# Weight pieces of an attention-and-experts kernel copied by VectorE or ScalarE as the list scheduler places them, with other weights for its due times

## The chip, the cores and the metric

The kernel runs on one core of one Trainium2 chip. The metric is the device time of one execution in microseconds (us), the median of several runs; lower is better. The engines are named as in the profile: PE is TensorE's matmul side and PEld its weight load, DVE is VectorE, ACT is ScalarE, POOL is GpSimd and SP is SyncE, which issues most DMAs here.

## The reference

Two parts follow one another. The first is an attention over channels, for 4 batches of 5056 tokens with 256 channels; the second is a mixture of 8 experts on its 20224 output rows, each row going to the expert with the highest gate logit.

```python
qn = q / (norm(q, axis=1) + 1e-6); kn = k / (norm(k, axis=1) + 1e-6)
s = kn.transpose(0, 2, 1) @ qn / tau            # 256 x 256 for each batch
a = softmax(s)
x = (v @ a).reshape(B * N, C)                   # 20224 x 256
logits = x @ w_gate; e = argmax(logits)         # 8 experts
out[row] = gate_w * (relu(x[row] @ w1[e]) @ w2[e])   # 256 -> 1024 -> 256
```

## The kernel before, in words

**The expert blocks.** Rows that the attention has produced are scattered by POOL to a DRAM array `xs` that has a region for each expert. Whenever a stage of the attention is complete (`ENDS`, L33: after some groups of 512 tokens, two in batch 0 and three in each later batch), a table (L509 on) is computed that says which expert and which 256 rows each of the next blocks takes. There are 72 blocks of 256 rows in 11 stages (`SURE` is 5, 12, 18, 26, 32, 38, 46, 52, 58, 66, 72 blocks, counted up) and 18 blocks of 128 rows for the rest. A block (L615 on) loads its rows transposed (`xT`, L609) and a small tile `mt` (L611) by SP, and multiplies in float16 parts: every number is a high and a low half, and three products stand for one.

**The pieces.** All weights lie in SBUF as float16 halves in `W`. Which expert a block needs is known on the chip alone, so its weights are copied from `W` at a register's address into a tile `wp` of 128 x 1024 (`piece`, L627): 8 pieces a block, 4 for the first matrix product (`first`, L631, PE L640 into PSUM tile `hp`) and 4 for the second (`second`, L655, PE L664 into `y`). The register is loaded once a block by `expert` (L621). There are 5 `wp` buffers (`WP`), so a piece can be made when PE has finished with the piece five back. In the kernel before, every piece is a VectorE copy (L629). ScalarE takes the ReLU of `hp` into the high half of `ht` (L648), VectorE makes the low half (L651), ScalarE scales `y` into `o` (L678) and POOL scatters `o` to the output (L682).

**The side work.** While the blocks of one stage run, the attention of the next groups goes on beside them: loads of q and k chunks, norms (`nraw`, ACT L1274, 20 loads of 512 KB for each of batches 1 to 3), halves of the chunks (`hl`, ACT L168 and DVE L175), score products (`sp`, PE L205 and L206), a softmax of small steps for each batch, and for each group of 512 tokens four products `px` (PE L1142), copies `xg` (ACT L1148), squares (ACT L1154), rows (ACT L364, DVE L368), the choice of the expert (DVE L388 to L398), counts (`r_ex`, DVE L411 and L412), ranks (`rtp`, PE L417 and L420) and four scatters (POOL L456).

**What sets the order.** All engines run in order, and the order is made ahead of time by a list scheduler (`task` L703, `lay` L717): every step is a task with an engine, a planned cost in us, the tasks it needs and a rank. `lay` repeatedly takes the task that could begin first by the planned times; among tasks that could begin at once, the one with the lower rank. A task is begun as soon as its engine is free and its inputs are there, so the rank only says who goes first; it holds nothing back. A piece is planned at 0.45 us of VectorE, `expert` at 0.4. PE's steps that read another engine's result are planned 0.4 us behind it, some 1.0 us (`LEAD`).

**The due times.** The ranks are due times. L973 to L1008 give every step of side work a weight (for a group of batch 1 to 3: 4 x 1.9 for its products and 0.5 for its rank), add these up, and spread them over the numbered blocks so that a stage's weights are done `EARLY` = 2 blocks before its rows are wanted (a hull of points of block number and summed weight). A step's due time (`due`, L1017) is read off that line; a block's steps have theirs from the block's number (`block_due`, L1020).

Of the kernel before, what the change touches and what calls it, by code (L numbers as in the profile page):

```python
# [18 lines left out]
ENG = mybir.EngineType  # L19

P = 128
B, N, C = 4, 5056, 256
NP = 5120
E, F = 8, 1024
# [5 lines left out]
T = 4  # L30
# [38 lines left out]
def attention_then_experts(ctx, tc, qk, qkc, vT, wts_in, kc, out):  # L69
# [89 lines left out]
    WP = 5  # L159
# [454 lines left out]
    def block(stage, tab, i, load):  # L614
        nt = P if stage == LAST else BLK  # L615
        nj = nt // P
        nf = 512 // nt
        wps, hps, hts, ys = {}, {}, {}, []
        b = {}

        def expert():  # L621
            b["e"] = nc.values_load(
                tab()[0][0:1, i : i + 1], engines=[ENG.DVE], min_val=0, max_val=E - 1,
                skip_runtime_bounds_check_because=WHY,
            )

        def piece(n):  # L627
            wps[n] = work.tile([P, 1024], F16, tag="wp", name="wp", bufs=WP)
            vec.tensor_copy(out=wps[n], in_=Wf[:, ds(b["e"] * 8192 + n * 1024, 1024)])  # L629

        def first(k):  # L631
            wp = wps.pop(k).rearrange("p (d s f) -> p d s f", d=2, s=2)
            xT = load()[0]
            for f in (2 * k, 2 * k + 1):
                if f % nf == 0:
                    hps[f // nf] = ps_h.tile([P, nf, nt], F32, tag="hp", name="hp")
                n = 0
                for dc in range(2):
                    for wh, xh in ((0, 0), (0, 1), (1, 0)):
                        pe.matmul(  # L640
                            hps[f // nf][:, f % nf, :], wp[:, dc, wh, (f % 2) * P : (f % 2 + 1) * P],
                            xT[:, 2 * xh + dc, :], start=(n == 0), stop=(n == 5),
                        )
                        n += 1

        def relu(h):
            hts[h] = work.tile([P, 2, nf, nt], F16, tag="ht", name="ht", bufs=4)
            act.activation(hts[h][:, 0], hps[h], AF.Relu)  # L648

        def rest(h):  # L650
            vec.scalar_tensor_tensor(  # L651
                out=hts[h][:, 1], in0=hps.pop(h), scalar=0.0, in1=hts[h][:, 0], op0=ALU.max, op1=ALU.subtract
            )

        def second(k):  # L655
            if k == 0:
                both = ps_y.tile([P, 2, C], F32, tag="y", name="y", bufs=2)
                ys.extend(both[:, j, :] for j in range(nj))
            wp = wps.pop(4 + k).rearrange("p (f s d) -> p f s d", f=2, s=2)
            for f in (2 * k, 2 * k + 1):  # L660
                for j in range(nj):
                    n = 0
                    for hh, wh in ((0, 0), (0, 1), (1, 0)):
                        pe.matmul(  # L664
                            ys[j], hts[f // nf][:, hh, f % nf, j * P : (j + 1) * P], wp[:, f % 2, wh, :],
                            start=(f == 0 and j == 0 and n == 0), stop=(f == 7 and j == nj - 1 and n == 2),
                        )
                        n += 1

        def factor():  # L670
            b["fac"] = tiny.tile([P, 2], F32, name="b_fac")[:, 0:nj]
            vec.tensor_scalar(
                out=b["fac"], in0=load()[1][:, :, 0], scalar1=fe[:, ds(b["e"], 1)], scalar2=None, op0=ALU.mult
            )

        def result(j):
            b["o", j] = work.tile([P, C], F32, tag="o", name="o", bufs=2)
            act.activation(b["o", j], ys[j], AF.Copy, scale=b["fac"][:, j : j + 1])  # L678

        def store(j):  # L680
            stored(
                pool.indirect_dma_start(  # L682
                    out=out[:, :],
                    out_offset=bass.IndirectOffsetOnAxis(ap=load()[1].bitcast(I32)[:, j, 1:2], axis=0),
                    in_=b.pop(("o", j)), in_offset=None, bounds_check=NT - 1, oob_is_err=False,
                )
            )

        return nj, nf, expert, piece, first, relu, rest, second, factor, result, store
# [8 lines left out]
                    tc.declare_no_dep(raw, group=f"bank{t2}{other.engine}", reason="another bank")  # L698
        tc.add_to_no_dep_group(f"bank{t}{raw.engine}", raw)

    tasks, rings = {}, {}

    def task(name, engine, cost, deps, emit, rank, after=0.0, wire=0.0, takes=(), uses=(), on=()):  # L703
        deps = list(deps)
# [12 lines left out]
    def lay():  # L717
        needs, users = {}, {}
        for name, (_, _, deps, *_) in tasks.items():
            flat = set()  # L720
            for d in deps:
                flat.update(d if isinstance(d, list) else [d])
            flat.discard(name)
            for d in flat:
                users.setdefault(d, []).append(name)
            needs[name] = flat
        missing = [d for d in users if d not in tasks]
        assert not missing, missing
        open_, ready, free, ends, begun = {n: len(d) for n, d in needs.items()}, {}, {}, {}, []
        wire = 0.0  # L730

        def made_ready(name):
            engine = tasks[name][0]
            at = 0.0
            for d in needs[name]:
                end, other, seen = ends[d]
                at = max(at, end if other is engine else seen + (LEAD.get(name[:2], LEAD.get(name[0], 0.4)) if engine is pe else 0.0))
            ready.setdefault(engine, {})[name] = at

        for name, n in open_.items():  # L740
            if n == 0:
                made_ready(name)
        while any(ready.values()):
            best = None
            for engine, some in ready.items():
                now = free.get(engine, 0.0)
                for name, at in some.items():
                    key = (max(at, now), tasks[name][4], len(begun))
                    if best is None or key < best[0]:
                        best = (key, name)  # L750
            (at, _, _), name = best
            engine, cost, deps, emit, rank, after, carried = tasks[name]
            del ready[engine][name]
            end = at + cost
            if engine is not None:
                free[engine] = end
            seen = end + (0.25 if engine is pe else 0.12) + after
            if carried:
                wire = max(wire, end + after) + carried
                seen = wire + 0.6  # L760
            ends[name] = (end, engine, seen)
            begun.append((at, len(begun), name))
            for u in users.get(name, ()):
                open_[u] -= 1
                if open_[u] == 0:
                    made_ready(u)
        assert len(begun) == len(tasks), [n for n in tasks if n not in ends][:20]
        for _, _, name in sorted(begun):
            tasks[name][3]()
        return begun, ends  # L770

    by_hand = tc.manual_schedule(engines={pe.engine, act.engine, vec.engine, sync.engine})
# [68 lines left out]
    def call(f, *args):  # L841
        return lambda: f(*args)
# [136 lines left out]
    for b in range(B):  # L979
        side = []  # L980
        if b == 1:
            side += [(("norm", b, n), 0.0, 0.6) for n in range(20)]
        if b > 1:
            side += [(("chunk", b, ch), 1.31, 1.2) for ch in range(NCH)]
        if b:
            side += [(("soft", b), 3.0, 7.0)]
        for g in range(AHEAD if b == 0 else 0, G):
            side += [(("x", b, g, t), 0.68 if b else 0.89, 1.9 if b else 1.2) for t in range(T)] + [(("rank", b, g), 0.3, 0.5)]
        for what, cost, weight in side:
            amount[what] = total  # L990
            total += weight
            done_by.append(total)
            spent.append(spent[-1] + cost)
            if what[0] == "rank" and what[1:] in ENDS[1:]:
                bounds.append(total)
# [356 lines left out]
    def block_tasks(n):  # L1352
# [15 lines left out]
        many = 8 // nf  # L1368
        for k in range(4):
            yield  # L1370
            task(("piece", n, k), vec, 0.45, [("expert", n)], call(piece, k), d(2 * k + 1) - 2, takes=[("wp", WP)])
            opens, closes = 2 * k % nf == 0, (2 * k + 1) % nf == nf - 1
            task(("first", n, k), pe, whole, [("piece", n, k), ("load", n), "handed"] + ([("first", n, k - 1)] if k else []),
                 call(first, k), d(2 * k + 1), takes=[("hp", 3)] if opens else [], uses=[("wp", 0)] + ([] if opens else [("hp", 0)]))
# [6 lines left out]
        task(("factor", n), vec, 0.14, [("load", n), ("expert", n), "factors"], factor, d(10), takes=[("b_fac", 2)], on=[mts])  # L1381
        for k in range(4):
            yield
            task(("piece", n, 4 + k), vec, 0.45, [("expert", n)], call(piece, 4 + k), d(8 + 2 * k) - 2, takes=[("wp", WP)])
            h = (2 * k + 1) // nf
            task(("second", n, k), pe, 1.32 if nj == 2 else 0.66, [("piece", n, 4 + k), ("rest", n, h)] + ([("second", n, k - 1)] if k else []),
                 call(second, k), d(8 + 2 * k), takes=[("y", 2)] if k == 0 else [], uses=[("wp", 0)])
            hts[h].append(("second", n, k))
# [80 lines left out]
```

## Time and profile before

| | us |
|---|---|
| median of 3 runs | 1175.9 (1173.66 to 1176.03) |
| the profiled execution, its own time | 1175.05 |
| its span, first to last instruction | 1173.3 |
| PE busy | 1136.9 (97%) |
| DVE busy | 903.8 (77%) |
| ACT busy | 673.2 (57%) |
| POOL busy | 358.8 (31%) |

The busy times are unions of what each engine executed; waiting, register loads and semaphores are not in them. A matmul's recorded end lies behind the moment at which the next one may start, so an idle gap of PE looks somewhat shorter in the profile than the time that was lost.

### The profile page before, as it was taken

The page shows a single profiled execution, that of the slowest core. Times are in us where ns is not written, and L with a number is a line of the kernel's source. Part 1 is how long each engine was busy: PE and PEld are TensorE (multiplying, and loading weights), DVE is VectorE, ACT ScalarE, POOL GpSimd, SP SyncE. Part 2 cuts the span into 40 slices and gives each one's busy share as a digit, 9 for nine tenths or more (in the row PEclk, how much of TensorE's full clock was granted, in tenths as well). Part 3 has the DMA queues.
Part 4 walks back from the last instruction along what each step waited for, and adds up shares of the span by engine and source line. Part 5 has one row for each costly group of instructions (what it writes and reads, how often), then busy time and mean ns, then how long its engine had stood idle before and what let it go on. Part 6 is the DMA issues. An engine that isn't in the chain of part 4 may idle for free.

```text
span 1173.3 us, 28744 instructions
## 1 busy us (share of the span) xinstructions
PE 1136.9 (97%) x10325; PEld 992.6 (85%) x10325; DVE 903.8 (77%) x2624; ACT 673.2 (57%) x1475; POOL 358.8 (31%) x335
## 2 busy tenths in 40 slices
PE   9989999989999999999999999999999999999998
PEld 8878778878888777988878877888888888889997
DVE  5797676877778887787768797778788677767886
ACT  5575476577876555477776655466565443332332
POOL 0044432234343411143344321133343323322222
PEclk9999899999999999999999999999999999999999
DMA  9999679256764576255585366343342323322221
GB/s 368 408 405 333 170 232 258 79 166 179 201 183 112 131 201 178 56 154 145 172 217 156 103 187 190 83 101 96 97 115 67 73 55 61 79 60 48 45 47 35
DMA packets 155938, 177.40 MB, mean 151 GB/s; under 512 B 116972, under 2 KB 117233, under 8 KB 155792
## 3 DMA queue, kind: packets, MB, share of 16 engines
q1 hardware_dynamic: 139968, 132.74, 41.2%
q0 software_dynamic: 15824, 42.79, 10.7%
q8 instruction: 82, 1.34, 0.5%
q14 instruction: 64, 0.52, 0.1%
HBM read 111.48 MB, written 43.29 MB: 132 GB/s over the span
## 4 chain that ended last, share of the span: by engine, by line
PE 73%; issue 9%; DMA 7%; DVE 4%; ACT 3%; POOL 2%; another core or an unknown queue 1%; SPq 0%; POOLq 0%; DVEq 0%; ACTq 0%
PE hp L640 29%; PE y L664 29%; PE px L1142 6%; DMA raw<-in_qk 4%; DMA W<-in_w 3%; PE sp L205 3%; POOL out L682 2%; PE sp L183 2%; PE px L1054 2%; PE sp L206 1%; DVE hl L175 1%; ACT nraw L1274 1%; DVE ht L651 1%; DVE wp L629 1%
## 5 line engine op out<-in xcount | busy, mean ns | idle before, releaser
L640 PE MATMUL hp<-xT,wp 128*128 128x256 f16 (+1 forms) x4320 | 487.4, 263 | 9.2 <-issue 6.7
L664 PE MATMUL y<-wp,ht 128*128 128x256 f16 x3888 | 484.2, 273 | 7.9 <-issue 7.3
L640 PEld LDWEIGHTS <-wp 128*128 128x128 f16 x4320 | 390.6, 98 | 58.6 <-issue 10.8
L664 PEld LDWEIGHTS <-ht 128*128 128x128 f16 x3888 | 375.4, 98 | 56.2 <-issue 11.3
L629 DVE COPY wp<-W 128x1024 f16 x720 | 301.6, 436 | 118.3 <-PE hp L640 65.3
L648 ACT ACTIVATE ht<-hp 128x512 f16<-128x512 f32 x324 | 191.6, 593 | 274.2 <-PE hp L640 206.8
L682 POOL DMA_INDIRECT out<-o,mt x162 | 169.8, 1048 | 501.4 <-ACT o L678 462.3
L456 POOL DMA_INDIRECT xs<-rows,r_si x160 | 183.0, 1144 | 303.4 <-ACT W L143 69.7
L651 DVE SCALAR_TENSOR_TENSOR ht<-hp,ht 128x512 f16<-128x512 f32 x324 | 221.9, 685 | 49.6 <-ACT ht L648 41.4
L678 ACT ACTIVATE o<-y,b_fac 128x256 f32<-128x256 f32 x162 | 69.2, 469 | 53.8 <-PE y L664 25.0
L1142 PE MATMUL px<-a_h,hl 128*128 128x264 f16 x480 | 99.1, 276 | 0.4 <-DVE hl L175 0.3
L1142 PEld LDWEIGHTS <-hl 128*128 128x128 f16 x720 | 68.2, 98 | 12.3 <-issue 1.2
L168 ACT ACTIVATE hl<-raw,qk_s 128x512 f16<-128x512 f32 x80 | 53.3, 713 | 32.8 <-PE sp L206 25.1
L1148 ACT COPY xg<-px 128x264 f32<-128x264 f32 x128 | 47.5, 374 | 41.4 <-PE px L1142 14.2
L175 DVE SCALAR_TENSOR_TENSOR hl<-raw,qk_s,hl 128x512 f16<-128x512 f32 x80 | 56.2, 744 | 17.2 <-ACT hl L168 17.0
L1274 ACT ACTIVATE nraw<-nraw 128x1024 f32<-128x1024 f32 x60 | 63.1, 1052 | 6.9 <-DMA nraw<-in_qkc 5.0
L1142 PE MATMUL px<-a_l,hl 128*128 128x264 f16 x240 | 66.2, 276 | 0.2 <-issue 0.2
L364 ACT ACTIVATE rows<-xg,x_sc 128x256 f16<-128x256 f32 x128 | 56.0, 498 | 18.0 <-DVE x_sc L89 16.4
L1154 ACT ACTIVATE xjunk<-xg 128x256 bf16<-128x256 f32 x128 | 53.2, 416 | 3.0
L368 DVE SCALAR_TENSOR_TENSOR rows<-xg,x_sc,rows 128x256 f16<-128x256 f32 x128 | 54.3, 476 | 0.3 <-ACT rows L364 0.3
L205 PE MATMUL sp<-hl 128*128 128x512 f16 x160 | 54.2, 379 | 0.0
L206 PE MATMUL sp<-hl 128*128 128x256 f16 x160 | 43.6, 273 | 0.1
(186 smaller groups left out, 910.2 us busy)
## 6 DMA issues: line engine op xcount, KB each, us to landing
raw<-in_qk SPq DMA_DIRECT2D x80, 512.0 KB
nraw<-in_qkc SPq DMA_DIRECT2D x60, 512.0 KB
vraw<-in_vT SPq DMA_DIRECT2D x32, 512.0 KB
W<-in_w SPq DMA_DIRECT2D x28, 512.0 KB
v<-in_vT SPq DMA_DIRECT2D x16, 256.0 KB
out<-o,mt POOLq DMA_INDIRECT x162
xs<-rows,r_si POOLq DMA_INDIRECT x160
wraw<-in_w SPq DMA_DIRECT2D x4, 512.0 KB
```

What stands on the lines that cost most here:

```text
L175: vec.scalar_tensor_tensor(out=hl[:, 1, :, part], in0=raw[:, :, part], scalar=sc, in1=hl[:, 0, :, part], op0=ALU.mult, op1=ALU.subtract)
L205: pe.matmul(sp[c], hl[:, 0, j, kc0 : kc0 + P], hl[:, :, j, 0:C], start=first, stop=False)
L456: ins = pool.indirect_dma_start(out=xs[:, :], out_offset=bass.IndirectOffsetOnAxis(ap=si[:n, t : t + 1], axis=0), in_=rows[:n, t, :], in_o ...
L629: vec.tensor_copy(out=wps[n], in_=Wf[:, ds(b["e"] * 8192 + n * 1024, 1024)])
L640: pe.matmul(hps[f // nf][:, f % nf, :], wp[:, dc, wh, (f % 2) * P : (f % 2 + 1) * P], xT[:, 2 * xh + dc, :], start=(n == 0), stop=(n == 5),)
L648: act.activation(hts[h][:, 0], hps[h], AF.Relu)
L651: vec.scalar_tensor_tensor(out=hts[h][:, 1], in0=hps.pop(h), scalar=0.0, in1=hts[h][:, 0], op0=ALU.max, op1=ALU.subtract)
L664: pe.matmul(ys[j], hts[f // nf][:, hh, f % nf, j * P : (j + 1) * P], wp[:, f % 2, wh, :], start=(f == 0 and j == 0 and n == 0), stop=(f == ...
L678: act.activation(b["o", j], ys[j], AF.Copy, scale=b["fac"][:, j : j + 1])
L682: pool.indirect_dma_start(out=out[:, :], out_offset=bass.IndirectOffsetOnAxis(ap=load()[1].bitcast(I32)[:, j, 1:2], axis=0), in_=b.pop(("o ...
L1142: pe.matmul(pt, hl[:, vh, c, ts], ah[:, c, :], start=(n == 0), stop=(n == 5))
L1274: act.activation(raw, raw, AF.Square, accum_out=sums[b][:, n // 5, n % 5 : n % 5 + 1])
```

## The change

Five edits, all to the planned order and to who copies a piece:

- `piece` can be made by ScalarE. The first such piece of a block loads the expert's number into a register of ScalarE, in the order of ScalarE's own work.
- `lay` looks at every piece as a task of VectorE or of ScalarE. On ScalarE its start counts `SHY` = 0.8 us later than it could be, and its planned cost is `ACT_PIECE` = 0.95 us.
- Every piece of every block is given this choice. The rest of the block and the 5 buffers are as before.
- Weights of side work: the norms of batch 1 count 0.72 each for 0.6; a softmax 10 for 7; a product of batches 1 to 3 counts 1.5 for 1.9, or 2.0 in groups 3 to 7 of batches 1 and 2, beside which the norms of the next batch are loaded.
- The rank of a group counts 5.0 where a stage ends with it, and 0.2 elsewhere; before it was 0.5 everywhere.

```diff
-        def piece(n):
+        def piece(n, by=vec):
             wps[n] = work.tile([P, 1024], F16, tag="wp", name="wp", bufs=WP)
-            vec.tensor_copy(out=wps[n], in_=Wf[:, ds(b["e"] * 8192 + n * 1024, 1024)])
+            if by is vec:
+                vec.tensor_copy(out=wps[n], in_=Wf[:, ds(b["e"] * 8192 + n * 1024, 1024)])
+                return
+            if "a" not in b:
+                b["a"] = nc.values_load(
+                    tab()[0][0:1, i : i + 1], engines=[ENG.Activation], min_val=0, max_val=E - 1,
+                    skip_runtime_bounds_check_because=WHY,
+                )
+            act.copy(out=wps[n], in_=Wf[:, ds(b["a"] * 8192 + n * 1024, 1024)])
...
+    SHY, ACT_PIECE = 0.8, 0.95
...
-            engine = tasks[name][0]
-            at = 0.0
-            for d in needs[name]:
-                end, other, seen = ends[d]
-                at = max(at, end if other is engine else seen + (...))
-            ready.setdefault(engine, {})[name] = at
+            for engine, bias in ((tasks[name][0], 0.0), *((e, 1.0) for e in either.get(name, ()))):
+                at = 0.0
+                for d in needs[name]:
+                    end, other, seen = ends[d]
+                    at = max(at, end if other is engine else seen + (...))
+                ready.setdefault(engine, {})[name] = at + bias * SHY
...
-                    key = (max(at, now), tasks[name][4], len(begun))
+                    if name in either and engine is not tasks[name][0]:
+                        now_ = now + SHY
+                    else:
+                        now_ = now
+                    key = (max(at, now_), tasks[name][4], len(begun))
...
+            if mine is not engine:
+                at -= SHY
+                engine, cost = mine, ACT_PIECE
+            taken[name] = engine
...
-            side += [(("norm", b, n), 0.0, 0.6) for n in range(20)]
+            side += [(("norm", b, n), 0.0, 0.72) for n in range(20)]
...
-            side += [(("soft", b), 3.0, 7.0)]
+            side += [(("soft", b), 3.0, 10.0)]
...
-            side += [(("x", b, g, t), 0.68 if b else 0.89, 1.9 if b else 1.2) for t in range(T)] + [(("rank", b, g), 0.3, 0.5)]
+            heavy = 2.0 if 0 < b < B - 1 and 3 <= g < 8 else 1.5 if b else 1.2
+            side += [(("x", b, g, t), 0.68 if b else 0.89, heavy) for t in range(T)]
+            side += [(("rank", b, g), 0.3, 5.0 if (b, g) in ENDS else 0.2)]
...
-            task(("piece", n, k), vec, 0.45, [("expert", n)], call(piece, k), d(2 * k + 1) - 2, takes=[("wp", WP)])
+            either["piece", n, k] = [act]
+            task(("piece", n, k), vec, 0.45, [("expert", n)], lambda by, k=k: piece(k, by), d(2 * k + 1) - 2, takes=[("wp", WP)])
...
-            task(("piece", n, 4 + k), vec, 0.45, [("expert", n)], call(piece, 4 + k), d(8 + 2 * k) - 2, takes=[("wp", WP)])
+            either["piece", n, 4 + k] = [act]
+            task(("piece", n, 4 + k), vec, 0.45, [("expert", n)], lambda by, k=k: piece(4 + k, by), d(8 + 2 * k) - 2, takes=[("wp", WP)])
```

## Rows read from the trace of the kernel before

**Rows 1.** Busy time of each engine in six stretches of the span (us; number of instructions in brackets), TensorE's granted clock, mean DMA share and GB/s.

```profile
140.00:250.00 110.00, 106.83 (x945) 93.63 (x943) 80.43 (x250) 75.06 (x174) 31.38 (x30) 0.98 0.67 182
250.00:400.00 150.00, 140.99 (x1270) 122.02 (x1271) 115.74 (x395) 108.06 (x272) 57.96 (x55) 1.00 0.60 164
400.00:500.00 100.00, 98.61 (x829) 80.67 (x827) 79.21 (x193) 53.10 (x99) 19.78 (x18) 1.00 0.53 146
500.00:700.00 200.00, 194.49 (x1747) 167.75 (x1745) 161.45 (x533) 140.67 (x340) 76.05 (x70) 1.00 0.60 164
700.00:1000.00 300.00, 297.66 (x2692) 260.75 (x2691) 231.27 (x687) 163.05 (x382) 93.72 (x88) 1.00 0.38 94
1000.00:1173.30 173.30, 167.67 (x1959) 154.90 (x1956) 129.71 (x317) 52.20 (x96) 42.16 (x43) 1.00 0.22 52
```

**Rows 2.** What PE waited for from 140 us to the end: us in total, times, longest. "issue" is a gap before which no wait ended.

```profile
PE y L664 <- issue: 7.3, 13, 1.1
PE hp L640 <- issue: 6.7, 11, 1.1
PE hp L640 <- DVE wp L629: 2.3, 3, 1.2
PE rtp L420 <- DVE r_ex L411: 1.7, 5, 0.4
PE rtp L417 <- DVE r_oh L398: 1.2, 1, 1.2
PE y L664 <- DVE wp L629: 0.4, 1, 0.4
PE px L1142 <- DVE hl L175: 0.3, 1, 0.3
PE rtp L417 <- DVE r_r L394: 0.3, 1, 0.3
PE ctp L515 <- DVE r_sl L445: 0.3, 1, 0.3
```

**Rows 3.** PE in order of time at two places: start us, us, engine, line, operation, tiles, count, and in brackets the idle time before it. The second place is followed by the products behind it.

```profile
171.78 0.38 PE L640 MATMUL hp<-xT,wp 128*128 128x256 f16 x2 [1.15 <-issue]
173.21 0.38 PE L640 MATMUL hp<-xT,wp 128*128 128x256 f16 x2 [1.05 <-issue]
...
250.24 1.48 PE L640 MATMUL hp<-xT,wp 128*128 128x256 f16 x12 [1.22 <-DVE wp L629]
251.56 0.28 PE L1142 MATMUL px<-a_h,hl 128*128 128x264 f16 x1
```

**Rows 4.** The second product's matmuls (L664): count, and min, median and max duration in ns, first and last start.

```profile
L664 PE MATMUL y<-wp,ht x3888: 269/273/282, 149.6 to 1167.4; 128*128 128x256 f16 x195
```

**Rows 5.** VectorE in order of time before the late piece of 250.24 us.

```profile
248.16 1.68 DVE L368 SCALAR_TENSOR_TENSOR rows<-xg,x_sc,rows 128x256 f16<-128x256 f32 x4 [0.31 <-ACT rows L364]
249.76 0.76 DVE L629 COPY wp<-W 128x1024 f16 x2
```

**Rows 6.** ScalarE in order of time at the same place.

```profile
247.63 1.69 ACT L364 ACTIVATE rows<-xg,x_sc 128x256 f16<-128x256 f32 x4
249.23 0.20 ACT L439 ACTIVATE rows<-kt 128x4 int32<-128x4 f32 x1
249.32 0.82 ACT L678 ACTIVATE o<-y,b_fac 128x256 f32<-128x256 f32 x2
```

**Rows 7.** Groups of instructions by line: busy us, mean ns of one, idle time of the engine before them and what ended it.

```profile
L629 DVE COPY wp<-W 128x1024 f16 x720 | 301.6, 436 | 118.3 <-PE hp L640 65.3 <-PE px L1142 16.1 <-PE y L664 14.2
L648 ACT ACTIVATE ht<-hp 128x512 f16<-128x512 f32 x324 | 191.6, 593 | 274.2 <-PE hp L640 206.8 <-remote 17.5 <-PE px L1142 14.5
L1274 ACT ACTIVATE nraw<-nraw 128x1024 f32<-128x1024 f32 x60 | 63.1, 1052 | 6.9 <-DMA nraw<-in_qkc 5.0 <-issue 1.9
L168 ACT ACTIVATE hl<-vraw,v_s 128x1024 f16<-128x1024 f32 x30 | 34.4, 1148 | 4.3 <-DVE v_s L89 4.0
```

**Rows 8.** Instructions of the sequencers that belong to a piece or a register load: min, median and max ns, first and last start. L629's precede each piece, L622's are the loads of `expert`, L1410's is the one register load that ScalarE makes, at the end of the kernel.

```profile
L629 DVEq FUSED_REGOPS  x720: 65/69/75, 131.2 to 1163.7; - x180
...
L622 DVEq TENSOR_LOAD <-c_tb x90: 297/306/862, 130.6 to 1036.9; - x90
...
L1410 ACTq TENSOR_LOAD <-nb x1: 463/463/463, 1167.7 to 1167.7; - x1
```

**Rows 9.** The waits of pieces on VectorE that PE ended (us in total, times, longest).

```profile
DVE wp L629 <- PE hp L640: 65.3, 93, 2.7
...
DVE wp L629 <- PE px L1142: 16.1, 13, 3.4
...
DVE wp L629 <- PE y L664: 14.2, 18, 2.4
```

**Rows 10.** The pieces alone (L629): VectorE's busy time with them and their number in two stretches, clock and DMA.

```profile
250.00:400.00 150.00, 36.64 (x89) 1.00 0.60 164
...
500.00:700.00 200.00, 50.15 (x120) 1.00 0.60 164
```

**Rows 11.** What SP's queue waited for before it issued a block's load (L609) and before it read the table (L604).

```profile
SPq L609 <- PE hp L640: 92.5, 23, 8.9
...
SPq L604 <- DVE c_tb L578: 39.2, 5, 18.0
```

More of the change, by code (lines that the diff above doesn't have):

```diff
@@ L699, in bank @@
         tc.add_to_no_dep_group(f"bank{t}{raw.engine}", raw)
-    tasks, rings = {}, {}
+    tasks, rings, either, taken = {}, {}, {}, {}
+    SHY, ACT_PIECE = 0.8, 0.95
     def task(name, engine, cost, deps, emit, rank, after=0.0, wire=0.0, takes=(), uses=(), on=()):
@@ L732, in made_ready @@
         def made_ready(name):
-            engine = tasks[name][0]
-            at = 0.0
-            for d in needs[name]:
-                end, other, seen = ends[d]
-                at = max(at, end if other is engine else seen + (LEAD.get(name[:2], LEAD.get(name[0], 0.4)) if engine is pe else 0.0))
-            ready.setdefault(engine, {})[name] = at
+            for engine, bias in ((tasks[name][0], 0.0), *((e, 1.0) for e in either.get(name, ()))):
+                at = 0.0
+                for d in needs[name]:
+                    end, other, seen = ends[d]
+                    at = max(at, end if other is engine else seen + (LEAD.get(name[:2], LEAD.get(name[0], 0.4)) if engine is pe else 0.0))
+                ready.setdefault(engine, {})[name] = at + bias * SHY
         for name, n in open_.items():
@@ L747, in lay @@
                 for name, at in some.items():
-                    key = (max(at, now), tasks[name][4], len(begun))
+                    if name in either and engine is not tasks[name][0]:
[3 more added lines that the diff above has]
+                    key = (max(at, now_), tasks[name][4], len(begun))
                     if best is None or key < best[0]:
-                        best = (key, name)
-            (at, _, _), name = best
+                        best = (key, name, engine)
+            (at, _, _), name, mine = best
             engine, cost, deps, emit, rank, after, carried = tasks[name]
-            del ready[engine][name]
+            for e in (engine, *either.get(name, ())):
+                del ready[e][name]
+            if mine is not engine:
+                at -= SHY
+                engine, cost = mine, ACT_PIECE
+            taken[name] = engine
             end = at + cost
@@ L768, in lay @@
         for _, _, name in sorted(begun):
-            tasks[name][3]()
+            if name in either:
+                tasks[name][3](taken[name])
+            else:
+                tasks[name][3]()
         return begun, ends
```

## The prediction

> **What bounds the kernel now.** I read the stretches first, then PE's waits, then the places of these waits in order of time, and the groups of pieces last. From 140 us on the kernel is a stream of blocks, and PE is the engine that is never free: in the six stretches it is busy 1006.25 of 1033.3 us [rows 1]. Busy is not peak, so the pace has to be read too: twelve matmuls that begin at 250.24 are followed by the next at 251.56, which is 0.11 us for each, at a granted clock of 1.00 (2.4 GHz) [rows 1, 3], though each is recorded as 0.27 us long [rows 4]. PE is thus at its pace wherever it is busy, and the change takes no matmul away. It can win only from PE's 27.05 us of idle time.
>
> These divide in three. The last matmul starts at 1167.4 and PE's last busy time ends some 5.6 us before the end [rows 1, 4]: the last result, its scatter and the end of the program, which no edit touches. 14.0 us, 24 times, are gaps that no wait ended [rows 2]. Two of them stand inside one set of twelve matmuls, where nothing new can be waited for [rows 3]: I take these gaps for late instructions of PE itself. The third part is VectorE's: 2.3 + 0.4 us on pieces (4 waits) and 1.7 + 1.2 + 0.3 + 0.3 + 0.3 = 3.8 us on what the ranks, a half and a table need (9 waits) [rows 2]. Since a matmul's recorded end lies 0.27 - 0.11 = 0.16 us behind the next one's start, every wait costs about 0.16 more than its row says. So pieces cost 2.7 + 4 x 0.16 = 3.3 us, VectorE's other late results 3.8 + 9 x 0.16 = 5.2, together 8.5 us, 0.7% of the kernel. The gaps without a wait cost 14.0 + 24 x 0.16 = 17.8.
>
> Why VectorE is late can be seen at 250.24: PE waits 1.22 us for a piece that stands on VectorE behind four row halves of 1.68 us [rows 3, 5]. The plan counts a piece at 0.45 us; on the chip it is 0.436 plus 0.069 of register work, 0.505 [rows 7, 8], so eight pieces put VectorE 0.44 us behind its plan in every block; the register load (planned 0.4, 0.306 on the chip [rows 8]) gives 0.1 back.
>
> **The change, part by part.** *Pieces on ScalarE.* A piece goes there when VectorE could begin it more than 0.8 us later than ScalarE could. How many do, no row says. At least none; at most the 720 less the 93 + 13 + 18 = 124 for which VectorE was standing idle until PE freed the buffer [rows 9], so 596. I take 200, nearer the lower end, since 0.8 us is nearly two pieces and an idle ScalarE is wanted too. That frees VectorE of 200 x 0.505 = 101 us, a tenth of its load. On the path it is worth the late pieces, and part of the rest. Of the 3.3 us I take 2.7 (between 0, if the late pieces stay, and 3.3). Of the 5.2 I take half, 2.6 (between 0 and 5.2): these results wait in VectorE's order, which moves forward, but PE's place for them is planned forward too. Gain 5.3 us. What is late next is the gaps without a wait, which I leave as they are.
>
> *What it costs ScalarE.* No row shows a float16 copy of 1024 columns there. The nearest are 1.052 us (a square of 1024 columns) and 1.148 (a half with a scale from memory) [rows 7]; I take the first, which has no such scale, so 200 x 1.05 = 210 us. With each block's first such piece comes a register load of which the plan knows nothing; ScalarE's only one took 0.463 us, VectorE's 0.306 [rows 8], and I take ScalarE's own. With 0.07 of register work a piece, a block with three is some 0.7 us behind the plan. The cover is ScalarE's slack: it stands idle 206.8 us before ReLUs because PE has not finished [rows 7]. Behind a delayed ScalarE are queued the next ReLU, the low half that VectorE makes of it, and the second product; also the `xg` copies that free PSUM. I take 1.3 us of new PE waits (0 to 12; the upper end is the first rival's). Semaphores from a second engine to PE: PE already waits for two engines before one product; nothing.
>
> *The weights.* They change ranks, not costs, and since the scheduler holds nothing back, only who goes first. Batch 2 sums to 20 x 1.2 + 7 + 10 x (4 x 1.9 + 0.5) = 112 before and 24 + 10 + 5 x 8 + 5 x 6 + 3 x 5 + 7 x 0.2 = 120.4 after, over the same 20 blocks. A group that ends no stage took 8.1 / 5.6 = 1.45 blocks and takes 8.2 / 6.02 = 1.36 with norms beside it and 6.2 / 6.02 = 1.03 without; a stage's end has nearly a block more. Tables come earlier. On SP that moves block loads, vraw, nraw and chunk loads against each other, on POOL the scatters. Before, SP waited five times for a table, up to 18.0 us, and 92.5 us for a buffer of `xT` [rows 11], yet PE never waited for a load after 140 us [rows 2]: two blocks of lead hide both. If that cover went, a late load would stop PE for us at a time; ScalarE's waits on nraw loads, 5.0 us in 60 [rows 7], are the nearest row and I take 0. POOL is busy in under half of every stretch [rows 1]. The denser groups press both engines for a while, the emptier ends relieve them: I take 0, with 2 us to either side.
>
> **Sum.** -5.3 + 1.3 = -4.0 us. The profiled execution took 1175.05 us (span 1173.3), 0.85 below the median of 1175.9; on the median that is **1171.9 us**, 0.3% faster. A change of 0.2%, 2.4 us, is about what a measurement of this kernel can tell from none.
>
> **Rivals.**
> *ScalarE takes VectorE's place (slower).* In 250 to 400 and 500 to 700, where all of VectorE's waits fall, ScalarE is already busy 108.06 of 150 and 140.67 of 200 us [rows 1]: 101 us free. There are 89 + 120 = 209 pieces, 26 blocks [rows 10]. The register loads take 26 x 0.463 = 12 us, the rest holds 89 / 1.05 = 85 pieces. So beyond 4 pieces in 10 on ScalarE it is full there, and every 0.7 us a block by which it runs behind plan, 18 us in all, comes through to PE in some part. With half: +9 - 5.3 = +3.7, **1179.6 us**. Against it speaks that the scheduler counts 0.95 us of each 1.05 and chooses ScalarE only when it is free; for it, that at 250.24 ScalarE too was busy without a break from 247.63 to 250.14 [rows 6], so where VectorE is late ScalarE is not idle. [...]
>
> *The waits stay (no change).* Either few pieces move, because ScalarE is seldom free when VectorE is late, or the plan draws the rank products forward by as much as VectorE gains: 5.2 of the 8.5 us are not waits for a piece at all. Then -1, **1175 us**.
>
> *A larger gain.* All 8.5 us go and the gaps without a wait shrink by chance, because other DMA traffic falls beside them, by a tenth of 17.8: **1165.6 us**. Nothing in the edits aims at these gaps; they could as well grow.
>
> **How the numbers follow.** The forecast has 0.45, the larger gain 0.1, no change 0.25, ScalarE in the way 0.2. Range 1165.6 to 1179.6: from the larger gain to the slower rival, which includes the bounds of the pieces' gain and of the weights; some 2 in 10 lies beyond, slower more than faster. Faster by over 0.2%: 0.45 + 0.1 = 0.55; within: 0.25; slower: 0.2.
>
> **What would show it.** Right: some 200 copies `wp<-W` on ScalarE with mean near 1.05 us and one register load a block before them; VectorE's busy time down by about 87 us (200 x 0.436), ScalarE's up by about 210; PE's waits on `wp`, `r_ex`, `r_oh` together 3 us or less where they were 6.5; PE's time in the stretches 250 to 700 closer to full; the gaps without a wait near 14 us again. Wrong: new rows of PE waiting on ACT (pieces, `xg`, or `ht` behind a late ReLU) of over 3 us; fewer than 50 pieces on ScalarE; waits on loads `xT` or `mt`; or a change of several us in the gaps without a wait.

## The result, and the profile after

The changed kernel took **1182.44 us**, median of 6 runs (1180.66 to 1185.62), beside 1175.66 us (1172.85 to 1176.53) for the kernel before on the same chip: ratio 1.0065 [1.0046, 1.0084]. It is slower by 6.8 us where 4 us of gain were forecast. The profiled execution took 1183.11 us, its span is 1181.5.

One thing must be known for what follows. The kernel before took about 1175 us in two of the six comparisons of this study, 1165 in one and 1149 in three, each steady within it; the same chip showed 1149 in one and 1175 in another, so the level is not a chip's. Ratios are therefore only read within a comparison, and its level stands beside them. One run of `before_jerk` (2396.87 us) and one of `ends_only_held` (2809.3 us), far above all others, are left out of the ratios below.

The pieces first, by line (busy us, mean ns, idle time before them), then the sequencers' view of ScalarE's new register load (min, median and max ns, first and last start).

```profile
L630 DVE COPY wp<-W 128x1024 f16 x646 | 273.7, 439 | 115.5 <-PE hp L648 69.5
L637 ACT COPY wp<-W 128x1024 f16 x74 | 76.4, 1042 | 2.7 <-PE y L672 2.2
```

```profile
L633 ACTq TENSOR_LOAD <-c_tb x38: 272/277/547, 133.0 to 975.0; - x38
```

Only 74 of 720 pieces went to ScalarE, in 38 blocks. A copy takes 1042 ns there; the register load has a median of 0.277 us.

The six stretches, with the columns of [rows 1]:

```profile
140.00:250.00 110.00, 108.33 (x961) 95.41 (x962) 79.66 (x247) 78.23 (x177) 34.15 (x32) 0.98 0.67 179
250.00:400.00 150.00, 139.51 (x1257) 119.82 (x1256) 116.40 (x412) 114.94 (x281) 59.62 (x55) 1.00 0.61 167
400.00:500.00 100.00, 99.86 (x835) 81.13 (x834) 71.27 (x157) 69.45 (x117) 16.87 (x16) 1.00 0.52 145
500.00:700.00 200.00, 193.69 (x1748) 168.18 (x1746) 157.91 (x518) 154.09 (x356) 75.53 (x70) 1.00 0.60 164
700.00:1000.00 300.00, 292.60 (x2615) 253.63 (x2613) 219.47 (x656) 188.08 (x407) 92.45 (x86) 0.99 0.36 93
1000.00:1181.50 181.50, 175.51 (x2030) 161.94 (x2027) 133.65 (x318) 54.76 (x101) 43.87 (x45) 0.99 0.23 52
```

Up to 500 us PE is busy 1.3 us longer than in [rows 1]; from 700 to 1000 it is busy 292.60 us where it was 297.66. VectorE is less busy there too, 219.47 us where it was 231.27, so its load over the stretch does not explain what PE lost; the places have to be read.

PE's waits from 140 us to the end (us, times, longest), to set beside [rows 2]:

```profile
PE y L672 <- issue: 10.0, 17, 1.1
PE hp L648 <- DVE wp L630: 2.1, 2, 1.3
...
PE hp L648 <- issue: 1.9, 2, 1.4
PE rtp L420 <- DVE r_ex L411: 1.7, 4, 0.4
PE ctp L515 <- DVE r_sl L445: 1.6, 2, 0.9
...
PE px L1165 <- DVE hl L175: 1.4, 3, 0.9
...
PE rtp L417 <- DVE r_oh L398: 1.2, 4, 0.4
PE y L672 <- DVE wp L630: 1.0, 2, 0.6
PE rtp L417 <- DVE v_s L89: 1.0, 1, 1.0
```

The gaps without a wait ("issue") come to 14.6 us with the smaller rows (10.0 + 1.9 and two of 1.4 and 1.3), where they were 14.0. VectorE's late results come to 2.1 + 1.7 + 1.6 + 1.4 + 1.2 + 1.0 + 1.0 = 10.0 us in 18 waits, where they were 6.5 in 13. Pieces are late by 3.1 us now and 2.7 before: no gain there, and ranks, halves and tables went from 3.8 to 6.9. (A wait of 2.1 us for ScalarE's `xg` at 139.91, L1158, is left out: the kernel before has the same 2.06 us, at 138.59 us.)

Idle rows do not show all of a delay, so I also counted PE's lost time after 141 us from the starts of its matmuls, against their median pace, and sorted it by what stood before the late start:

| us lost | a wait for data had ended | no wait | half clock |
|---|---|---|---|
| before, 1175.05 | 8.9 | 20.6 | 1.9 |
| after, 1183.11 | 14.6 | 21.1 | 2.8 |

Half clock is time at a granted clock of 0.50, such as 141.0 to 144.5 us in the kernel before: its matmuls of 256 columns start 0.213 us apart there, and 0.109 at 1.00. The differences are +5.7, +0.5 and +0.9; with +1.0 ahead of 141 us and +0.3 at the end it comes to 8.4 us, where the two profiled executions differ by 8.1. The two differ most in 800 to 900 us, 9.6 us lost in the changed kernel and 0.4 in the kernel before. PE there, in order of time, and VectorE ahead of the first place:

```profile
811.54 0.18 PE L417 MATMUL rtp<-r_oh,tri 128*128 128x32 f16 x1 [1.00 <-DVE v_s L89]
...
812.33 0.92 PE L672 MATMUL y<-wp,ht 128*128 128x256 f16 x7 [0.59 <-DVE wp L630]
...
823.38 0.27 PE L672 MATMUL y<-wp,ht 128*128 128x256 f16 x1 [0.82 <-issue]
824.11 0.27 PE L672 MATMUL y<-wp,ht 128*128 128x256 f16 x1 [0.46 <-issue]
824.89 0.71 PE L672 MATMUL y<-wp,ht 128*128 128x256 f16 x5 [0.52 <-issue]
```

```profile
810.15 1.27 DVE L368 SCALAR_TENSOR_TENSOR rows<-xg,x_sc,rows 128x256 f16<-128x256 f32 x3
811.34 0.15 DVE L89 TENSOR_SCALAR v_s<-vtp 128x1 int32<-128x1 int32 x1
...
811.85 0.43 DVE L630 COPY wp<-W 128x1024 f16 x1
```

Two kinds of loss stand side by side. At 811.54 a rank product waits 1.00 us for a small step that VectorE reaches only behind three row halves (1.27 us), and the piece of the next product stands behind it (0.59 us). At 823 to 825 PE pauses three times inside one set of matmuls, and nothing waited for ends there. With such pauses go waits of VectorE and ScalarE for a completion signal of PE that comes 1.6 to 3.5 us after the end of the instruction that gives it, in this profile and in that of the kernel before ("remote").

```profile
ACT ht L656 <- remote: 19.2, 8, 4.0
...
ACT xg L1171 <- remote: 10.5, 3, 3.7
...
DVE wp L630 <- remote: 9.0, 3, 4.7
```

The kernel before has these rows too in its profile at this level: 17.5 us in 7 for `ht`, 9.4 in 4 for `xg`, 9.4 in 4 for `wp`. They are hardly a loss of their own kind: of 14 such waits after 141 us in the changed kernel 11 end within 0.3 us of the end of a PE gap without a wait, and 11 of 15 in the kernel before. VectorE and ScalarE at the place shown above:

```profile
824.98 0.43 DVE L630 COPY wp<-W 128x1024 f16 x1 [2.42 <-remote]
```

```profile
825.05 0.38 ACT L1171 COPY xg<-px 128x264 f32<-128x264 f32 x1 [3.75 <-remote]
```

### The profile page after: what moved, and what is told of

It reads as the page before. It is cut to its first block, busy times and chain, and to the rows that moved or that the text cites. A ratio compares the mean times of both kernels' runs of the same rounds, so it can differ in the third digit from the quotient of the medians.

```text
span 1181.5 us, 28742 instructions
## 1 busy us (share of the span) xinstructions
PE 1139.8 (96%) x10325; PEld 992.9 (84%) x10325; DVE 883.4 (75%) x2550; ACT 741.4 (63%) x1549; POOL 359.0 (30%) x335
## 3 DMA queue, kind: packets, MB, share of 16 engines
q8 instruction: 82, 1.34, 0.5%
## 4 chain that ended last, share of the span: by engine, by line
PE 76%; issue 9%; DVE 4%; DMA 4%; ACT 3%; POOL 2%; another core or an unknown queue 1%; POOLq 0%; ACTq 0%; DVEq 0%; SPq 0%
PE hp L648 30%; PE y L672 29%; PE px L1165 6%; PE sp L205 3%; DMA raw<-in_qk 2%; POOL out L690 2%; DMA W<-in_w 2%; PE sp L183 2%; PE px L183 2%; PE sp L206 2%; PE px L1077 1%; PE px L1158 1%; DVE hl L175 1%; DVE ht L659 1%
## 5 line engine op out<-in xcount | busy, mean ns | idle before, releaser
L630 DVE COPY wp<-W 128x1024 f16 x646 | 273.7, 439 | 115.5 <-PE hp L648 69.5
L637 ACT COPY wp<-W 128x1024 f16 x74 | 76.4, 1042 | 2.7 <-PE y L672 2.2
L1171 ACT COPY xg<-px 128x264 f32<-128x264 f32 x128 | 47.7, 374 | 39.5 <-PE px L1165 18.8
L168 ACT ACTIVATE hl<-raw,qk_s 128x512 f16<-128x512 f32 x80 | 53.2, 715 | 18.9 <-PE sp L206 18.5
```

What stands on the lines that cost most here:

```text
L637: act.copy(out=wps[n], in_=Wf[:, ds(b["a"] * 8192 + n * 1024, 1024)])
```

## Experiments

Theories. **P**: pieces on ScalarE cost what was gained. **W**: the new weights do, and among them **R**, the rank's weight (0.5 becoming 5.0 at a stage's end and 0.2 elsewhere). **L**: any redrawn order lands some microseconds better or worse. **S**: the new order is no worse by its plan, but bears delays that the plan does not know worse than the old one does. Where the rank's weight is set apart, **G** stands for the other new weights.

### The parts alone, and two nudges of the old weights (the kernel before: 1149.15 us)

`pieces_only` is the change with the old weights, `weights_only` the kernel before with the new ones. The nudges change one old weight a little:

```diff
-... + [(("rank", b, g), 0.3, 0.5)]
+... + [(("rank", b, g), 0.3, 0.6)]      # jitter_rank
-... 1.9 if b else 1.2) for t in range(T)]
+... 1.95 if b else 1.2) for t in range(T)]     # jitter_x
```

> The choice of engine for the pieces alone, with the weights of before. Theory W (the new weights cost the time, the pieces are harmless or help): 0 to -5 us against before, so 1171 to 1176. Theory P (pieces on ScalarE cost it): +5 to +8 us. Theory L (before is a lucky draw among orders that differ in small things, and any redrawn order loses): +3 to +8 us. Some 80 pieces on ScalarE are expected.

> The new weights alone, every piece on VectorE. Theory W: +6 to +11 us against before, with PE waits on ranks and halves of VectorE between 800 and 900 us as after the change. Theory P: within 2 us of before. Theory L: +3 to +8 us.

> Before with one neutral step: every rank counts 0.6 for 0.5. No due time moves by more than about 1 us against another. Theories W and P: within 2 us of before. Theory L: +3 to +8 us.

> Before with another neutral step: a product of batches 1 to 3 counts 1.95 for 1.9. Theories W and P: within 2 us of before. Theory L: +3 to +8 us; the spread between this, the other neutral step and before is then the size below which a change of order tells nothing.

| | us | ratio to the kernel before |
|---|---|---|
| pieces_only (83 pieces on ScalarE) | 1147.59 | 0.9988 [0.9974, 1.0002] |
| weights_only | 1148.80 | 1.0005 [0.9996, 1.0015] |
| jitter_rank | 1148.31 | 0.9999 [0.9987, 1.001] |
| jitter_x | 1150.02 | 1.0009 [0.9998, 1.0019] |

No part costs anything here, and L shows at most 0.1%. But the kernel before itself was 26 us quicker than in the first comparison, so both kernels were run again unchanged.

### Both kernels again (1149.23 us)

> The whole change once more, beside before on one chip. In the first comparison before took 1175.7 us and had 18 us of PE gaps without a wait; in the comparison of the parts before took 1149.2 and PE had under 2 us of such gaps. Theory S (the loss of 6.8 us needs the late instructions of the first comparison: every engine then falls behind the plan in jerks, and the new order has less room for that): where before is near 1149, within 2 us of before or up to 3 faster; where before is near 1175, +5 to +8 us. Theory I (the two parts cost nothing alone and 6 to 7 us together, by their order): +5 to +8 us wherever it runs. By the parts alone (ratios 0.9988 and 1.0005) the sum would be -1 us.

> The kernel before, with a profile, as the control for all that is compared with it: ratio 1.000 by every theory. Where its time is near 1149 us, theory S expects PE gaps without a wait of under 3 us after 140 us and no waits of VectorE or ScalarE that end by an unknown queue (9 and 27 us in the first profile); where it is near 1175, as in the first profile.

The change took 1150.34 us, ratio 1.0005 [0.9995, 1.0015], the unchanged kernel 1149.63, 1.0006 [0.9994, 1.0019]: **at this level the whole change is worth nothing.** PE's waits after 140 us, before_again and after_again, all of the first kernel's and the largest two of the other's:

```profile
PE rtp L420 <- DVE r_ex L411: 1.5, 1, 1.5
PE hp L640 <- DVE wp L629: 1.4, 2, 0.8
PE hp L640 <- DVE c_tk L544: 0.8, 1, 0.8
PE ctp L515 <- DVE r_sl L445: 0.2, 1, 0.2
```

```profile
PE hp L648 <- DVE wp L630: 1.7, 3, 0.8
PE y L672 <- DVE wp L630: 0.7, 2, 0.5
```

There is no gap without a wait and no late signal, and VectorE's late results are 3.9 us in 5 waits. The profiled executions of the kernel before at the two levels lie 27.8 us apart (1175.05 and 1147.28); the matmul starts give 20.6 of this to these gaps, and 3.7 to data that came late. So the 1175 us level is for the most part the plan plus gaps without a wait and late signals, and the loss under study was seen only among them. That is what S says; P and W as costs that need no disturbance are out. Whether the order as such or the places where the gaps fell made the loss is not yet told.

### Hold-ups of the sequencers (the kernel before: 1165.06 us)

Four kernels were to get register loads that hold PE, ScalarE and VectorE in 23 blocks:

```diff
+        def held_up(engine, times):
+            for _ in range(times if jerk else 0):
+                nc.values_load(tab()[0][0:1, i : i + 1], engines=[engine], ...)
```

> Before, with unplanned hold-ups in every third 256-row block (23 blocks): 2 register loads on PE ahead of its second piece's matmuls (0.6 us each), 6 on ScalarE behind a ReLU (0.28 us each) and 7 on VectorE behind the low half (0.31 us each), in the place of the late instructions and late signals of the first comparison. The plan knows nothing of them. PE's own hold-ups give 23 x 1.2 = 28 us; with waits for a late VectorE or ScalarE +28 to +40 us against before without hold-ups.

> The whole change with the same hold-ups. Theory S (the new order bears unplanned delays worse): slower than before with the same hold-ups by 3 to 9 us. Theory C (the first comparison's loss has a cause that hold-ups of this kind don't bring out, such as where late instructions happen to fall): within 2 us of before with hold-ups.

> The new weights alone, with the same hold-ups. Theory S with the weights as what makes the order tight (denser groups, ranks planned 5 to 17 us earlier): slower than before with hold-ups by 3 to 9 us. Theory S with the pieces as the cause, and theory C: within 2 us.

> The choice of engine alone, with the same hold-ups. Theory S with the pieces as the cause (ScalarE fuller, its register loads unplanned): slower than before with hold-ups by 3 to 9 us. Theory S with the weights, and theory C: within 2 us, or up to 3 us faster.

These hold-ups did not come about: the registers are unused and the loads are gone from the program; only semaphore waits are left. before_jerk, ScalarE's and PE's (min, median, max ns):

```profile
L623 ACTq EVENT_SEMAPHORE  x138: 17/17/17, 177.7 to 1031.9; - x138
L623 PEldq EVENT_SEMAPHORE  x46: 51/51/51, 176.2 to 1030.8; - x46
```

So these are nearly the plain kernels, at a level with gaps of its own (14.1 us lost without a wait in before_jerk). That makes them a second look at the first comparison:

| | us | ratio | lost to late data |
|---|---|---|---|
| before_jerk | 1168.27 | 1.0021 [1.0004, 1.0037] | 10.0 |
| pieces_only_jerk | 1168.59 | 1.0021 [1.0004, 1.0037] | 7.9 |
| after_jerk | 1175.88 | 1.0093 [1.0076, 1.011] | 13.7 |
| weights_only_jerk | 1178.00 | 1.0116 [1.0095, 1.0137] | 16.9 |

**The new weights carry the loss, with or without the pieces**; the pieces with the old weights cost nothing beside before_jerk. That speaks against P as the cause of the loss, and against L in one draw: the order of pieces_only_jerk is redrawn as well. PE's waits, before_jerk, weights_only_jerk and pieces_only_jerk:

```profile
...
PE hp L649 <- DVE wp L636: 2.9, 4, 1.2
...
PE rtp L420 <- DVE r_ex L411: 1.9, 5, 0.4
```

```profile
...
PE hp L649 <- DVE wp L636: 4.5, 4, 1.4
...
PE ctp L515 <- DVE r_sl L445: 1.5, 3, 0.7
```

```profile
...
PE hp L657 <- ACT wp L644: 2.9, 2, 2.7
...
PE rtp L420 <- DVE r_ex L411: 1.0, 3, 0.4
PE y L685 <- ACT wp L644: 1.0, 1, 1.0
```

With the new weights the late pieces and table counts grow (2.9 to 4.5, and 0.5 to 1.5 for the table). By the matmul starts 6.9 us more were lost to late data (16.9 against 10.0), and 4.4 more without a wait (18.5 against 14.1): part of the 10.9 us between these two profiled executions (9.7 by the medians) is the disturbance itself, the larger part is data that came late. With the pieces alone two things cancel: VectorE's late results fall from 7.7 us in 15 waits to 2.2 in 7, and PE waits 4.2 us in 4 for ScalarE, where before_jerk has no such wait.

### Delays made on purpose, and the weights apart (the kernel before: 1148.96 us)

In every third block of 256 rows (23 blocks) the first ReLU and VectorE's low half of it are done four times, which holds ScalarE for 3 x 0.59 and VectorE for 3 x 0.69 us that the plan does not know (their means in the kernel before, 593 and 685 ns):

```diff
-            act.activation(hts[h][:, 0], hps[h], AF.Relu)
+            for _ in range(1 + 3 * (held and h == 0)):
+                act.activation(hts[h][:, 0], hps[h], AF.Relu)
...
```

`ends_only_held` has of the new weights the rank's alone, `rest_only_held` all of them but the rank's.

> Before, with real hold-ups: in every third 256-row block (23 blocks) the first ReLU is done four times over on ScalarE and its low half four times over on VectorE, so 1.5 us of ScalarE (23 x 3 x 0.5 = 34 us) and 1.8 us of VectorE (23 x 3 x 0.61 = 42 us) of which the plan knows nothing. The outputs are the same. PE's matmuls are unchanged. Both theories: +5 to +25 us against before, all of it PE waiting for VectorE.

> The new weights with the same hold-ups. Theory S (the order that the new weights make bears unplanned delays worse, on any chip): slower than before with hold-ups by 4 to 12 us. Theory H (the loss needs the late instructions of particular chips and the place where they fall; delays of VectorE and ScalarE alone don't bring it out): within 3 us of before with hold-ups where the chip is a fast one.

> Of the new weights the rank's alone (5.0 where a stage ends, 0.2 elsewhere), with the same hold-ups. Theory R (ranks and tables planned 5 to 17 us earlier put PE's rank and count products close behind a late VectorE): most of what the new weights lose. Theory G (lighter, so denser, groups of products lose it): within 3 us of before with hold-ups.

> The other new weights (products 1.5 or 2.0, softmax 10, norms 0.72) with the rank's weight 0.5 as before, with the same hold-ups. Theory G: most of what the new weights lose. Theory R: within 3 us of before with hold-ups.

| | us | ratio |
|---|---|---|
| before_held | 1182.35 | 1.0279 [1.0253, 1.0304] |
| rest_only_held | 1181.10 | 1.0276 [1.0255, 1.0297] |
| weights_only_held | 1190.55 | 1.0365 [1.0335, 1.0396] |
| ends_only_held | 1195.24 | 1.0374 [1.0347, 1.0401] |

The same delays cost the old weights 2.8% and the new ones 3.7%, at a level without gaps of its own: delays of VectorE and ScalarE are enough to bring the loss out. **Under them the rank's weight alone makes the whole difference.** PE's waits, before_held and then ends_only_held:

```profile
PE hp L640 <- DVE wp L629: 12.4, 10, 3.1
PE ctp L515 <- DVE r_sl L445: 4.0, 3, 1.8
```

```profile
PE hp L640 <- DVE wp L629: 18.3, 15, 2.4
PE rtp L417 <- DVE v_s L89: 6.4, 1, 6.4
```

Late pieces of the first product go from 10 waits to 15 (with those of the second product, from 15.6 us in 15 to 18.8 in 17), and one rank product, at 344.63 us, stops PE for 6.4 us. In the stretch of this stop, 250 to 400 us, the granted clock is 0.98 in the first kernel and 0.95 in the second, a mean over the stretch; PE is busy 6.1 us less there.

```profile
250.00:400.00 150.00, 140.76 (x1262) 123.02 (x1260) 124.80 (x407) 114.53 (x279) 58.68 (x56) 0.98 0.58 161
```

```profile
250.00:400.00 150.00, 134.64 (x1191) 116.70 (x1190) 118.77 (x384) 109.26 (x265) 60.34 (x54) 0.95 0.61 160
```

### The rank's weight undone in the change (the kernel before: 1175.82 us)

```diff
-            side += [(("rank", b, g), 0.3, 5.0 if (b, g) in ENDS else 0.2)]
+            side += [(("rank", b, g), 0.3, 0.5)]        # after_no_ends
```

`after_no_ends` has no hold-ups; `after_held` is the change with them, and `after_no_ends_held` has both edits. `lead_a_held` is the change with hold-ups, and the products for ranks and table counts planned 2.5 us behind what they read, where it was 1.0 for ranks and 0.4 for counts:

```diff
+    LEAD |= {..., "ctp": 2.5} | {("rank", b): 2.5 for b in range(1, B)}
```

> The change with one part undone: the rank counts 0.5 everywhere, as before; the choice of engine and the other new weights stay. No hold-ups. If the rank's weight is what costs the time: on a chip where before takes over 1160 us no slower than before (ratio 0.995 to 1.002, where the whole change had 1.0065 and 1.0093); on a faster one the same as before or up to 3 us faster (0.997 to 1.001). If it is the choice of engine together with any new weights: 1.005 to 1.010 on a slow chip.

> The whole change with the hold-ups on ScalarE and VectorE (23 blocks). Before had 1.0279 and the new weights alone 1.0365 against before without hold-ups. The choice of engine takes some load off VectorE: 1.030 to 1.037 if the order of the new weights is what bears delays badly; under 1.028 if the choice of engine makes up for it.

> The change without its rank weight, with the hold-ups. If the rank's weight is the cause: 4 to 12 us faster than the whole change with hold-ups, and no slower than 1.028 against before. If not: within 3 us of it.

> The whole change with the hold-ups, and PE's rank and count products planned 2.5 us behind VectorE where it was 1.0 and 0.4. If the loss is PE standing at rank and count products that were planned close behind a late VectorE: 4 to 10 us faster than the whole change with hold-ups, and PE's waits at those products under 4 us. If it is pieces and halves that come late because VectorE does the ranks and tables first: within 3 us of it.

| | us | ratio |
|---|---|---|
| after_no_ends | 1182.64 | 1.0055 [1.0036, 1.0073] |
| after_held | 1221.96 | 1.0389 [1.0362, 1.0416] |
| after_no_ends_held | 1210.28 | 1.0285 [1.0261, 1.0308] |
| lead_a_held | 1217.14 | 1.0353 [1.0329, 1.0376] |

With hold-ups the change behaves as the weights did: without its rank weight it is 11.7 us faster, the third pair that agrees (ends_only_held lies 12.9 us above before_held, weights_only_held 9.5 above rest_only_held). In the profiles of this pair, though, the matmul starts put only 2 of the 7.7 us between the two executions to late data and 7 to gaps without a wait, so here the times speak and not the profiles. More planned distance before rank and count products alone gains 4.8 us, with intervals that overlap a little; PE's waits at these products fall from 11.1 us to 3.1. But **without hold-ups, at the level of the first comparison, undoing the rank's weight does not take the loss away**: 1.0055, beside 1.0065 for the change itself in the first comparison, with overlapping intervals. The profile of after_no_ends says in part why. VectorE's late results are 7.7 us in 16 waits, where the change had 10.0 and the kernel before 6.5, but one wait has come in. PE, and ScalarE ahead of it:

```profile
169.51 1.47 PE L648 MATMUL hp<-xT,wp 128*128 128x256 f16 x12
175.09 1.25 PE L648 MATMUL hp<-xT,wp 128*128 128x256 f16 x5 [4.11 <-ACT wp L637]
```

```profile
173.51 0.60 ACT L656 ACTIVATE ht<-hp 128x512 f16<-128x512 f32 x1 [4.02 <-remote]
174.00 1.04 ACT L637 COPY wp<-W 128x1024 f16 x1
```

ScalarE stands at a ReLU for 4.02 us, until a signal of PE that comes late (the set before it ends at 170.98 us); the piece is next in its order, and PE stands for that piece. The changed kernel's profile has no such wait, but it is no accident of one execution: after_no_ends_held has it at 175.62 us (4.16) and pieces_only_jerk at 173.53 (2.70), the orders with pieces on ScalarE and the old rank weight. The kernel before has a late signal at nearly the same time (ScalarE's ReLU at 173.32 waits 3.97 us for it), and no piece stands behind it. So R is shown for the delays that I made; at the natural level undoing it lowered VectorE's late results and exposed a late piece of ScalarE. Without the 4.1 us after_no_ends would be near 1178.5 us, an estimate from one profile, so R's share there stays open.

## Why the prediction was wrong

**The bound** was right: PE's pace decides, at 0.11 us a matmul, and only its idle time is at stake. The 2.4 that the prediction sets beside a clock of 1.00 is the pace that the trace gives: in the kernel before, 12 matmuls of 256 columns (1085.33 us, L664) take 1.31 us from start to start and the 24 of 128 columns behind them (L640) 1.34 us, at a granted clock of 1.00, so 128 columns more take 0.053 us, 2.4 columns a ns.

**The gain of 5.3 us** did not come in the changed kernel. 74 pieces went to ScalarE, not 200; VectorE's load fell by 20 us, not 87. Late pieces cost 3.1 us by rows after 2.7, and the other late results rose from 3.8 to 6.9. With the old weights it did come, by rows: at 1165 us VectorE's late results fell by 5.5 us (pieces_only_jerk, 7.7 to 2.2), and ScalarE's late pieces took it back. Alone and at the level without gaps, the pieces measured 1.4 us of gain (0.9988), with an interval that reaches no change. There the kernel before's late results of VectorE are 3.9 us in 5 waits, with 0.16 for each 4.7 where I had 8.5: nearly half of what the gain was taken from was seen only in the disturbed execution, and I read it as the kernel's own.

**ScalarE's cost of 1.3 us** was no loss in the changed kernel: PE waited for no ScalarE piece there. With the old rank weight it was mis-sized: 4.2 us in pieces_only_jerk, 4.1 in one wait of after_no_ends, inside the range of 0 to 12 that was given. PE's waits on ScalarE were foreseen, with a full ScalarE as their cause; in that wait of after_no_ends a late signal of PE made ScalarE late. The duration holds (1042 ns taken as 1.05 us), the register load was too dear (0.463 taken, 0.277 measured).

**The weights: "I take 0, with 2 us to either side". This is the step that failed.** It is right where nothing is late (1.0005 [0.9996, 1.0015]). Among gaps without a wait and late signals it is wrong: with the kernel before at 1165 us, 1.0116 for the weights beside 1.0021 for before_jerk, both with the old copying, about 10 us. The fault is in the ground given, that weights change who goes first and not costs. Who goes first decides how much room a result has before PE wants it, and a delay uses up this room: by times the held kernels show that (1.0279 for the old weights, 1.0365 for the new ones). Beside it stands a second fault, the gaps "which I leave as they are". By rows they did stay (14.0 and 14.6 us), but I treated them as a fixed toll; that they are late instructions of PE was my reading, and no run shows what makes them. Most of the late signals to VectorE and ScalarE come with PE's gaps, and each is an unplanned delay on which the order is tried; the answer was late data, 14.6 us for 8.9.

**The rivals.** The slower one named a time near the measured one, by another mechanism. ScalarE did not fill up with half of the pieces, it took a tenth; PE waited for its pieces in after_no_ends (4.1 us), pieces_only_jerk (2.9 + 1.0), after_no_ends_held (5.0) and lead_a_held (1.1), not in the changed kernel. For a copy the changed kernel has 1042 ns on ScalarE against 439 on VectorE, and the runs show that this price did not decide. No change, the second rival, is what happened at the level of 1149 us. It was not reckoned that both could be true of one kernel. The larger gain did not come; that the gaps turn on the DMA traffic beside them was a guess of mine, and no run shows it.

**What stays open.** Under made delays the rank's weight is shown to be the cause; at 1165 us, among delays that occur by themselves, it is shown that the new weights as a whole are, and not which part. The 1175 us of the forecast itself was not taken apart so: after_no_ends alone ran there. A rank weight of 5.0 gives a stage's end more blocks and the groups before it fewer, so that rows, ranks and pieces meet on VectorE more densely; that this density is the mechanism at the natural level was argued, not shown. The two nudges were not run at that level nor with made delays, so some share of L is not excluded, beyond the one redrawn order that lost nothing. No version beat both kernels by more than its interval: pieces_only at 0.9988 [0.9974, 1.0002] is the nearest.

## What to carry to other kernels

An order made ahead of time has two qualities, its planned length and the room it leaves before each result is wanted, and the first says nothing of the second: try a new order with delays put in on purpose beside the old one with the same delays. Before explaining idle time in a profile, run the unchanged kernel once more: 26 us of 1175 were gone in other comparisons of the same program, and with them nearly half of the waits that looked like the change's prize. A change of 0.5% needs its control in the same comparison, and at both levels if there are two.

## What the runs showed of the hardware

The same program on the same chip ran at 1149 us in one comparison and 1175 in another. In the two profiles of the first comparison PE pauses up to 1.4 us with nothing to wait for, and VectorE and ScalarE wait up to 4.7 us for completion signals of PE, which the records put 1.6 to 3.5 us behind the end of the last instruction that gives one. The records are thinner there as well: of VectorE's 2371 semaphore updates 2084 are in the profile of the kernel before, and its DMA issues have no landing times (in before_again 11 of 14 rows have them). The row of the same 80 loads, of the kernel before and of before_again (KB each, median us to landing):

```profile
raw<-in_qk SPq DMA_DIRECT2D x80, 512.0 KB
```

```profile
raw<-in_qk SPq DMA_DIRECT2D x80, 512.0 KB, 4.8
```

What makes PE pause, or the level slower, no run here tells.
